# All pieces of w_in loaded before the first recurrence step, and merged transfers for the transposed inverses and the Gram rows, in a fused delta-rule attention and two-MLP kernel

## The chip, the cores and the metric

One core of one Trainium2 chip runs the whole program. The metric is the device time in microseconds of one execution; the kernel before was timed in three runs.

## What is computed

Four batches of eight heads (sequence 768, head width 48) go through a delta rule, and its 3072 rows of 384 features through two MLPs. Cut to what matters:

```python
# attention, per batch and head, t = 0..767
k_n = k / (norm(k) + 1e-6)
y[t]  = q[t] @ state
state = state + beta[t] * outer(k_n[t], v[t] - state.T @ k_n[t])
# first MLP: d_ff = 1024
h = x @ w_in;  solu = h * softmax(h)
x1 = ((solu - mean) / sqrt(var + 1e-6) * g_ln) @ w_out
# second MLP: d_ff = 2048
out = maximum(x1 @ w2_in, 0)**2 @ w2_out
```

The weights arrive as 64-bit floats and everything else as 32-bit floats.

## The kernel before, in words

**Attention.** The 768 tokens of a head are cut into 12 chunks of 64. A *step* t (24 of them, `NT`) holds one chunk of 16 heads-and-batches: 128 partitions by 2 sets by 4 pairs. Steps 0 to 11 and 12 to 23 are two independent recurrences. For every step, **e(t)** multiplies keys with queries and keys (L657); ScalarE puts the negated key-by-key Gram matrix into `g` (L683), which goes to the scratch `gscr` in DRAM, and the masked query part goes to `m`. e runs up to ten steps ahead (`LA`).

A chunk needs the inverse of a 64 by 64 triangular matrix. Its two diagonal 32 by 32 blocks are inverted by forward substitution (`inversion`) for a *group* of four steps at once, all 128 partitions in use, after the blocks have been loaded from `gscr` (into `ia` for group 0, into `it` for the others). The inversion of group 0 runs on VectorE, those of groups 1 to 5 on GpSimd (L886, L868, pairs of L905 and L922, L947 at the end). `it` is stored to `tscr`; ScalarE makes a transposed copy `ia` (L964), which is stored to `uscr`.

`load_tb(t)` brings the pieces of step t back: `g12` (Gram rows), `tbd` (inverses) and `t2` (transposed inverses). The off-diagonal block then takes **prep 1(t)** on TensorE (L1064, g12 by tbd), its copy `ys` by ScalarE (L1070), **prep 2(t)** (L1080, t2 by ys) and four copies into `tbd` (L1093). **z(t)** (L1107) multiplies the finished inverse into m, evacuated to `zs` (L1121). The recurrence itself is **a(t)** (state by keys and queries, L1134 and L1135; none for t = 0 and 12), the residual `r` on VectorE (L1150, or L1152 for t = 0 and 12, from the scaled `vt`), **o(t)** (L1164 and L1165) and the new state `s` (L1180, L1182). The output goes to `xt`.

**First MLP.** **Front(t)** transposes xt (L1206), splits it into a high and a low part `xh`, `xl`, and multiplies with the split w_in: 18 matmuls L1217 into `p_h`, three per 128 by 512 piece of w_in. VectorE takes the row maximum `sc` (L1232), ScalarE the exponential (L1240), VectorE the product with h (L1250); only then is `p_h` free for the next front. **Back** transposes the result (L1319); **out**, for every two fronts, multiplies it with the split w_out (72 matmuls L1339).

**The weights of the first MLP.** `load_w` loads one raw 64-bit piece into one of three `raw` buffers (512 KB for a piece of w_in, 384 KB for one of w_out) and converts it: ScalarE takes the magnitude into one of five `wst` buffers (L453), and four VectorE operations (L461, L472, L487, L497) build the 32-bit float. ScalarE then casts the high part (`w1h`, or `wgh` after a scaling, L534) and GpSimd subtracts for the low part (`w1l`, `wgl`, both L420). VectorE's part may not start before the inversion of group 0 is over (`first_inv`). w_in has six pieces, w_out eight. Two pieces of w_in are loaded before the first `load_tb`, the other four behind it.

**Second MLP.** Its 64-bit weights are converted to DRAM scratch through the same buffers during the attention, and it runs when the attention is over, from about 480 us on.

**What sets the order.** Every operation is added to a `Plan` with a cost, keys that it reads and writes, and a priority from the table `PR`. The plan runs a list scheduler forward and backward over these costs and writes every engine's instructions out in the order found; on the chip each engine then runs its own list strictly in order and waits with semaphores. All transfers go through SyncE (L300), on one hardware queue, in the plan's order.

Of the kernel before, what the change touches and what calls it, by code (L numbers as in the profile page):

```python
# [9 lines left out]
F32 = mybir.dt.float32  # L10
F32R = mybir.dt.float32r
U32 = mybir.dt.uint32
# [6 lines left out]
P = 128  # L19
C = 64  # L20
HB = 32
# [3 lines left out]
NP = 4  # L25
NCH = 12
NST = NB * NCH
GS = 8

G0 = (0, 4, 8, 12, 16, 20, 24)  # L30
NG = len(G0) - 1
# [8 lines left out]
TINY = 1e-36  # L40
RS0 = 2.0**-65.47
LA = 10
NRAW, NWST = 3, 5

F64_LO = 2.0**-15
F64_HI = 2.0**17 * (1 - 2.0**-24)
# [2 lines left out]
def group(t):  # L49
# [5 lines left out]
PR = {  # L55
    "prep": -0.96,
    "z": 0.04,
    "chain": 0.0,
    "e": 0.25,
    "evac": -0.46,  # L60
    "norms": 0.63,
    "inv": -10.66,
    "mf": -1.26,
# [199 lines left out]
def c_dve(n, fast=False):  # L263
    return 0.07 + n / (1920.0 if fast else 960.0)
# [12 lines left out]
def tile_delta_moe_moe(  # L277
# [14 lines left out]
    v, act, pool, pe = nc.vector, nc.scalar, nc.gpsimd, nc.tensor  # L292
# [5 lines left out]
    def dma(dst, src, r=(), w=(), prio=0.0, size=0):  # L298

        return add("sp", 0.06, lambda: nc.sync.dma_start(dst(), src()), r, w, prio, size, gate)  # L300
# [5 lines left out]
    dpool = ctx.enter_context(tc.tile_pool(name="dpool", bufs=1, space=DRAM))  # L306
# [9 lines left out]

    gscr = [dpool.tile([P, GS, NP, C], F32, name=f"gscr{g}") for g in range(NG)]
    tscr = [dpool.tile([4, GS, NP, HB, HB], F32, name=f"tscr{g}") for g in range(NG)]
    uscr = [dpool.tile([4, GS, NP, HB, HB], F32, name=f"uscr{g}") for g in range(NG)]
    x1scr = [dpool.tile([P, 3, 2 * P], F32, name=f"x1scr{i}") for i in range(NT // 2)]  # L320
    w2s = [dpool.tile([P, F2], F32, name=f"w2s{c}") for c in range(3)]
    wos = [dpool.tile([P, DM], F32, name=f"wos{f}") for f in range(16)]
# [40 lines left out]
    ez_ = bufs(m1, [P, F1], "ez", 2)  # L363
# [15 lines left out]
    tbd_ = bufs(ap_, [P, 2 * NP, C], "tbd", 3)  # L379
    t2_ = bufs(ap_, [P, NP, HB], "t2", 2)  # L380
    g12_ = bufs(ap_, [P, 2 * NP, HB], "g12", 2)
    ys = ap_.tile([P, NP, HB], F32, name="ys")
    zs_ = bufs(ap_, [P, NP, 112], "zs", 2)
    R = ap_.tile([P, 2, NP, D], F32, name="r")
    S = ap_.tile([P, 2, NP, D], F32, name="s")
    sqr = [P, HB, HB]
    ia = ap_.tile(sqr, F32, name="ia")
# [6 lines left out]
    raw_ = bufs(ap_, [P, 512, 2], "raw", NRAW, U32)  # L394
# [12 lines left out]
    if 2 * (T2 - T1) < GS:  # L407
        pool.memset(it_[1], 0.0)

    for t in (*tbd_, S, *g12_):  # L410
        pool.memset(t, 0.0)

    def split(hi, lo, src, n, r, w, prio, lo_eng="dve", fast=False):
# [16 lines left out]

    def load_w(src, n, prio):

        i, j = n_w[0] % NWST, n_w[0] % NRAW
        n_w[0] += 1
        w = wst_[i][:, 0:n]
        kw, kr = ("A", "wst", i), ("A", "raw", j)
        if src.dtype == F32:
            dma(lambda: w, lambda: src, (), [kw], prio - 1, P * n * 4)
            return w, kw
        raw, wu = raw_[j][:, 0:n], w.bitcast(U32)  # L440
        up, low = raw[:, :, 1], raw[:, :, 0]
        dma(
            lambda: raw.rearrange("p n t -> p (n t)"),
            lambda: src.bitcast(U32),
            (),
            [kr],
            prio - 1,
            P * n * 8,
        )
        add(  # L450
            "act",
            c_act(n, True),
            lambda: act.activation(out=w, in_=up.bitcast(F32), func=AF.Abs),  # L453
            [kr],
            [kw],
            prio,
        )
        add(
            "dve",
            c_dve(n),  # L460
            lambda: v.scalar_tensor_tensor(  # L461
                out=w, in0=w, scalar=F64_LO, in1=const(3, n), op0=ALU.max, op1=ALU.min
            ),
            [],
            [kw],
            prio,
            after=[*first_inv, *w2_gate],
        )
        add(
            "dve",  # L470
            c_dve(n),
            lambda: v.scalar_tensor_tensor(  # L472
                out=wu,
                in0=wu,
                scalar=3,
                in1=const(5, n, True),
                op0=ALU.logical_shift_left,
                op1=ALU.bitwise_and,
            ),
            [],  # L480
            [kw],
            prio,
        )
# [25 lines left out]
        return w, kw

    def load_w1i(i0, i1, prio):
        for i in range(i0, i1):
            c, n = divmod(i, 2)
            s = slice(n * 512, n * 512 + 512)
            w, kw = load_w(w1i[c, :, s], 512, prio)
            split(
                lambda c=c, s=s: w1h[:, c, s],
                lambda c=c, s=s: w1l[:, c, s],
                lambda w=w: w,
                512,  # L520
                [kw],
                [("W", "w1h", c, n), ("W", "w1l", c, n)],
                prio,
                "pool",
            )
# [303 lines left out]

    def inversion(g, en, prio):  # L830

        eng, cost = (v, lambda n, full=True: c_dve(n)) if en == "dve" else (pool, c_pool)
        gm = gm_[g % 2]
        it, itmp = it_[g % 2], junk[:, 512:] if g == 1 else itmp_
        kgm, kic, kia = ("A", "gm", g % 2), ("A", "itc", g % 2), ("A", "ia")
# [60 lines left out]
        for j in range(1, HB - 1):  # L896
# [69 lines left out]
            [kia, *(kraws if g == 0 else ())],  # L966
            prio,
        )
        dma(
            lambda: uscr[g].rearrange("h g p r s -> (h g p) r s"),  # L970
            lambda: ia,
            [kia],
            [("A", "uscr", g)],
            prio,
            P * 4096,
        )

    def load_tb(t, prio):

        g, tg = group(t)  # L980
        s0 = 2 * tg
        tb, t2, g12 = tbd_[t % 3], t2_[t % 2], g12_[t % 2]
        ktb, kt2, kg12 = ("A", "tbd", t % 3), ("A", "t2", t % 2), ("A", "g12", t % 2)
        for h in range(2):
            o = h * C
            dma(
                lambda o=o: g12[o : o + HB],
                lambda o=o: gscr[g][o : o + HB, s0 : s0 + 2].rearrange("r s p c -> r (s p) c")[
                    :, :, HB:
                ],  # L990
                [("A", "gscr", g, s) for s in (s0, s0 + 1)],
                [kg12 + (h,)],
                prio - 1,
                2 * HB * 1024,
            )

        def blk(scr, hb):
            return scr[g][hb, s0 : s0 + 2].rearrange("s p r c -> r (s p) c")

        for hb in (0, 2, 1, 3):  # L1000
            o, c = hb * HB, hb % 2 * HB
            last = dma(
                lambda o=o, c=c: tb[o : o + HB, :, c : c + HB],
                lambda hb=hb: blk(tscr, hb),
                [("A", "tscr", g)],
                [ktb + (hb,)],
                prio - 1,
                2 * 32 * 1024,
            )
        for h in range(2):  # L1010
            for e in range(2):
                o = (2 * h + e) * HB
                dma(
                    lambda o=o: t2[o : o + HB],
                    lambda h=h, e=e: uscr[g][2 * h + 1, s0 : s0 + 2].rearrange(
                        "s (k e) r c -> e r (s k) c", e=2
                    )[e],
                    [("A", "uscr", g)],
                    [kt2 + (h, e)],
                    prio - 1,  # L1020
                    2 * 32 * 512,
                )
        return last

    def load_kv(t, prio):
# [31 lines left out]
    def prep1_mm(t):  # L1057
        tb, g12 = tbd_[t % 3], g12_[t % 2]

        def mm():  # L1060
            for u in range(2 * NP):
                for h in range(2):
                    o, q = h * C, (2 * h + u % 2) * HB
                    pe.matmul(yp[q : q + HB, u // 2], g12[o : o + HB, u], tb[o : o + HB, u, 0:HB], start=True, stop=True)  # L1064

        r = [*(("A", "g12", t % 2, h) for h in range(2)), *(("A", "tbd", t % 3, 2 * h) for h in range(2))]
        return mm, r, [("A", "a")]

    def prep1_out(t, prio):
# [2 lines left out]
    def prep2_mm(t):  # L1072
        t2 = t2_[t % 2]

        def mm():
            for u in range(2 * NP):
                for h in range(2):
                    q = (2 * h + u % 2) * HB
                    s = slice(q, q + HB)
                    pe.matmul(yp[s, u // 2], t2[s, u // 2], ys[s, u // 2], start=True, stop=True)  # L1080

        return mm, [("A", "ys"), *(("A", "t2", t % 2, h, e) for h in range(2) for e in range(2))], [("A", "a")]

    def prep2_out(t, prio):
        tb = tbd_[t % 3]
# [493 lines left out]

    gate.append(wr)  # L1580
    inversion(1, "pool", PR["inv1"])
    load_w1i(0, 2, PR["w1i"])
    for t in range(T2, LA):
        e_tile(t, PR["e1"] + t * PR["e1s"])
        norms(t, PR["n2"])
# [10 lines left out]
    load_tb(1, PR["prep0"] + 2)  # L1596
    load_kv(1, PR["prep0"] + 2)
    prep_z(1, PR["prep0"] + 2, (1,))
    load_w1i(2, 6, PR["w1i"])
    load_w1o(PR["w1o"])  # L1600
    for t in range(NT + 3):
        if t < NT:
# [149 lines left out]
```

## Time and profile before

| | |
|---|---|
| Three runs | 905.94, 906.82, 912.15 us; median 906.82 |
| The profiled execution | 916.59 us, of which the span is 914.9 us |
| TensorE busy | 817.2 us (89% of the span) |
| VectorE, ScalarE, GpSimd busy | 499.5, 449.9, 311.2 us |
| Mean granted TensorE clock | 0.946 |
| DMA | 99.72 MB in 126576 packets, 84225 of them under 512 bytes |

A line of the page names an engine, a line of the kernel and the tiles. "Idle before" is the time the engine stood still before an instruction, with what released it. TensorE's clock (PEclk) is a share of 2.4 GHz; at 0.5 it runs at 1.2 GHz.

### The profile page before, as it was taken

How to read it: one execution, taken by the hardware profiler on the slowest of the kernel's cores; microseconds unless marked ns; L12 is line 12 of the kernel's file. 1: busy time of each engine (PE TensorE's matmuls, PEld its weight loads, DVE VectorE, ACT ScalarE, POOL GpSimd, SP SyncE). 2: the span in 40 equal slices, each digit the busy share in tenths (PEclk: the TensorE clock that was granted, in tenths of full speed). 3: DMA queues.
4: the chain of work that ended last, by engine and by line, in shares of the span. 5: the costliest groups of instructions: out<-in, count | busy, mean ns of one | idle time of the engine just before them, and what ended most of it. 6: DMA issues, size and time to landing. Idle time of an engine off the chain costs nothing.

```text
span 914.9 us, 24277 instructions
## 1 busy us (share of the span) xinstructions
PE 817.2 (89%) x9904; PEld 757.4 (83%) x9904; DVE 499.5 (55%) x984; ACT 449.9 (49%) x996; POOL 311.2 (34%) x759
## 2 busy tenths in 40 slices
PE   5425858999979889988999999999999999999997
PEld 4324647888868677787888999999999999999997
DVE  4994898543875875665657454343433333343332
ACT  2313587685766656475667444343333334343333
POOL 4389978757988957930000000000000000000000
PEclk9975877999999998998999999999999999999999
DMA  9826887456786775556434421010100101010101
GB/s 229 216 73 173 220 232 196 133 156 149 196 266 168 206 205 148 158 155 160 145 93 142 113 79 52 1 53 1 39 14 1 52 1 52 1 27 1 27 1 26
DMA packets 126576, 99.72 MB, mean 109 GB/s; under 512 B 84225, under 2 KB 106753, under 8 KB 126465
## 3 DMA queue, kind: packets, MB, share of 16 engines
q1 hardware_dynamic: 126464, 98.18, 39.2%
q8 instruction: 77, 1.26, 0.6%
q14 instruction: 35, 0.28, 0.1%
HBM read 69.83 MB, written 28.31 MB: 107 GB/s over the span
## 4 chain that ended last, share of the span: by engine, by line
PE 66%; DVE 12%; DMA 7%; POOL 4%; ACT 4%; issue 3%; SPq 3%; ACTq 0%; DVEq 0%; POOLq 0%
PE acc L1526 21%; PE h L1482 21%; PE p_x L1339 7%; PE p_h L1217 7%; SPq L300 3%; PE p_tr L1319 2%; PE p_a L1134 2%; DVE wst L461 2%; DVE itmp L905 2%; POOL it L922 1%; POOL itmp L905 1%; DVE it L922 1%; DVE wst L487 1%; DMA raw<-in_w1i_dram 1%; PE p_u L1107 1%
## 5 line engine op out<-in xcount | busy, mean ns | idle before, releaser
L1503 DVE TENSOR_TENSOR xt<-xt 128x384 f32<-128x384 f32 x128 | 71.5, 559 | 166.4 <-ACT xt L1495 166.3
L1495 ACT ACTIVATE xt<-h 128x384 f32<-128x384 f32 x128 | 62.8, 491 | 166.3 <-PE h L1482 165.9
L1482 PE MATMUL h<-x1l,w2h 128*128 128x384 f32 x384 | 128.7, 335 | 0.0
L1482 PE MATMUL h<-x1h,w2h 128*128 128x384 f32 x384 | 128.6, 335 | 0.0
L1482 PE MATMUL h<-x1h,w2l 128*128 128x384 f32 x384 | 128.5, 335 | 0.0
L1339 PE MATMUL p_x<-zh,wgh 128*128 128x256 f32 x288 | 87.3, 303 | 5.8 <-ACT xo L1353 5.4
L922 POOL TENSOR_TENSOR it<-it,itmp 128x72 f32<-128x72 f32 (+37 forms) x204 | 88.2, 448 | 4.5
L1526 PE MATMUL acc<-woh,xh 128*128 128x384 f32 x258 | 87.7, 340 | 0.9 <-ACT ot L1548 0.9
L905 POOL TENSOR_TENSOR itmp<-it 128x72 f32<-128x72 f32 (+37 forms) x204 | 86.9, 441 | 2.0
L1526 PE MATMUL acc<-wol,xh 128*128 128x384 f32 x258 | 87.4, 339 | 0.0
L1526 PE MATMUL acc<-woh,xl 128*128 128x384 f32 x258 | 87.1, 338 | 0.0
L1339 PE MATMUL p_x<-zh,wgl 128*128 128x256 f32 x288 | 83.2, 289 | 2.2 <-issue 2.2
L1339 PE MATMUL p_x<-zl,wgh 128*128 128x256 f32 x288 | 83.4, 290 | 0.3 <-DVE zl L420 0.3
L420 DVE TENSOR_TENSOR xl<-xt,xh 128x384 fp32r<-128x384 f32 x86 | 48.0, 558 | 44.8 <-ACT xh L415 44.4
L1482 PEld LDWEIGHTS h<-x1h,w2h 128*128 128x128 f32 x384 | 72.1, 188 | 0.0
L1482 PEld LDWEIGHTS h<-x1h,w2l 128*128 128x128 f32 x384 | 72.1, 188 | 0.0
L1482 PEld LDWEIGHTS h<-x1l,w2h 128*128 128x128 f32 x384 | 72.1, 188 | 0.0
L415 ACT CAST xh<-xt 128x384 fp32r<-128x384 f32 x86 | 44.1, 513 | 48.2 <-DVE xt L1503 47.2
L1217 PE MATMUL p_h<-w1h,xh 128*128 128x512 f32 x144 | 64.5, 448 | 2.6 <-DVE xl L420 2.6
L1339 PEld LDWEIGHTS p_x<-zh,wgh 128*128 128x128 f32 x288 | 56.4, 196 | 9.2 <-ACT xo L1353 6.2
L1217 PE MATMUL p_h<-w1l,xh 128*128 128x512 f32 x144 | 59.6, 414 | 0.0
L1217 PE MATMUL p_h<-w1h,xl 128*128 128x512 f32 x144 | 59.4, 413 | 0.0
(179 smaller groups left out, 1985.4 us busy)
## 6 DMA issues: line engine op xcount, KB each, us to landing
kql<-in_kin_dram SPq DMA_DIRECT2D x22, 512.0 KB, 5.1
kqe<-in_kin_dram SPq DMA_DIRECT2D x38, 192.0 KB, 3.0
raw<-in_w2i_dram SPq DMA_DIRECT2D x12, 512.0 KB, 5.3
raw<-in_w2o_dram SPq DMA_DIRECT2D x16, 384.0 KB
gscr<-g SPq DMA_DIRECT2D x21, 256.0 KB, 5.8
m<-in_ktok_dram SPq DMA_DIRECT2D x24, 192.0 KB, 6.8
vt<-in_vtok_dram SPq DMA_DIRECT2D x24, 192.0 KB, 3.9
x1scr<-xo SPq DMA_DIRECT2D x12, 384.0 KB, 3.7
```

The lines of the kernel that those rows point to most:

```text
L300: return add("sp", 0.06, lambda: nc.sync.dma_start(dst(), src()), r, w, prio, size, gate)
L415: add("act", c_act(n), lambda: act.copy(hi(), src()), r, [w[0]], prio)
L420: lambda: le.tensor_tensor(out=lo(), in0=src(), in1=hi().bitcast(F32), op=ALU.subtract),
L461: lambda: v.scalar_tensor_tensor(out=w, in0=w, scalar=F64_LO, in1=const(3, n), op0=ALU.max, op1=ALU.min),
L905: lambda tm=tm, j=j, nr=nr, w_=w_, c0=c0, c1=c1: eng.tensor_tensor(out=tm, in0=it[:, j + 1 :, j : j + 1].to_broadcast([P, nr, w_]), in1=it ...
L922: lambda tm=tm, j=j, c0=c0, c1=c1: eng.tensor_tensor(out=it[:, j + 1 :, c0:c1], in0=it[:, j + 1 :, c0:c1], in1=tm, op=ALU.add,),
L1217: pe.matmul(p_h[:, sl], xx[:, c], ww[:, c, sl], start=(c == 0 and k == 0), stop=(c == 2 and k == 2),)
L1339: pe.matmul(p_x1[:, 0 : 2 * P], ww[:, f, c * P : c * P + P], zz[:, f], start=(f == 0 and k == 0), stop=(f == 7 and k == 2),)
L1482: pe.matmul(late["h2", ih], late[ww][:, c, s], xx[:, c], start=(c == 0 and k == 0), stop=(c == 2 and k == 2),)
L1495: lambda: act.activation(out=rt, in_=late["h2", ih], func=AF.Relu),
L1503: lambda: v.tensor_tensor(out=gg, in0=rt, in1=rt, op=ALU.mult),
L1526: pe.matmul(late["acc", a], gg[:, a * P : a * P + P], late[ww][:, f], start=(f == 0 and k == 0), stop=(f == 15 and k == 2),)
```

## The change

- **w_in:** all six raw pieces are loaded ahead of the first `load_tb`. Pieces 0 to 3 go to four `raw` buffers (`NRAW` 3 to 4), pieces 4 and 5 to `ez_0` and `ez_1`, which hold inputs of e(4) and e(5) before and the first MLP's exponentials later. There are four `wst` buffers instead of five.
- **Transposed inverses:** `uscr` is laid out as t2 needs it. The store is two transfers of 128 KB (only the two blocks that are used) in pieces of 128 bytes, where it was one of 512 KB in pieces of 4 KB. t2 of a step is one transfer of 128 rows of 512 bytes, where it was four with pieces of 128 bytes.
- **Gram rows:** g12 of a step is one transfer over all 128 partitions (128 KB, half of it unused rows), where it was two of 32 KB. g12 is no longer set to zero at the start.
- **Plan:** the cost that the plan reckons for a VectorE operation of an inversion is 0.09 higher. `PR` is unchanged.

```diff
-NRAW, NWST = 3, 5
+NRAW, NWST = 4, 4
...
-    uscr = [dpool.tile([4, GS, NP, HB, HB], F32, name=f"uscr{g}") for g in range(NG)]
+    uscr = [dpool.tile([P, GS * NP // 2, HB], F32, name=f"uscr{g}") for g in range(NG)]
...
-    for t in (*tbd_, S, *g12_):
+    for t in (*tbd_, S):
...
-        i, j = n_w[0] % NWST, n_w[0] % NRAW
+        i, j = n_w[0] % NWST, n_w[0] - NRAW
         n_w[0] += 1
         w = wst_[i][:, 0:n]
-        kw, kr = ("A", "wst", i), ("A", "raw", j)
+        if 0 <= j < 2:
+            raw, kr = ez_[j].bitcast(U32).rearrange("p (n t) -> p n t", t=2)[:, 0:n], ("ez", j)
+        else:
+            j = (j - 2) % NRAW if j > 0 else j + NRAW
+            raw, kr = raw_[j][:, 0:n], ("A", "raw", j)
+        kw = ("A", "wst", i)
...
-        eng, cost = (v, lambda n, full=True: c_dve(n)) if en == "dve" else (pool, c_pool)
+        eng, cost = (v, lambda n, full=True: c_dve(n) + 0.09) if en == "dve" else (pool, c_pool)
...
-        dma(
-            lambda: uscr[g].rearrange("h g p r s -> (h g p) r s"),
-            lambda: ia,
...
+        for h in range(2):
+            o = (2 * h + 1) * HB
+            dma(
+                lambda h=h: uscr[g][rows[h]].rearrange("(e r) k c -> k e r c", e=2),
+                lambda o=o: ia[o : o + HB],
...
-        for h in range(2):
-            o = h * C
-            dma(
-                lambda o=o: g12[o : o + HB],
...
+        dma(
+            lambda: g12,
+            lambda: gscr[g][:, s0 : s0 + 2, :, HB:].rearrange("r s p c -> r (s p) c"),
...
-        for h in range(2):
-            for e in range(2):
-                o = (2 * h + e) * HB
-                dma(
-                    lambda o=o: t2[o : o + HB],
...
+        dma(
+            lambda: t2,
+            lambda: uscr[g][:, s0 * NP // 2 : s0 * NP // 2 + NP],
...
     inversion(1, "pool", PR["inv1"])
-    load_w1i(0, 2, PR["w1i"])
+    load_w1i(0, 6, PR["w1i"])
...
-    load_w1i(2, 6, PR["w1i"])
     load_w1o(PR["w1o"])
```

The plan writes a new order for every engine. Line numbers of the changed kernel are up to five off those of the kernel before (L457 to L953 are five higher there, L1044 and later two or three lower).

**SyncE's queue, the stretch ahead of the load of group 1's Gram blocks** (`it_1<-gscr1`), first as it stands before:

```order
L300 DMA raw_0_213<-in_w1i_dram 128x1024
L300 DMA gscr1_76<-g_1_178 128x512
L300 DMA kqe_0_175<-in_kin_dram 48x1024 x2
L300 DMA gscr1_76<-g_0_177 128x512
L300 DMA kqe_1_176<-in_kin_dram 48x1024
L300 DMA raw_1_214<-in_w1i_dram 128x1024
L300 DMA kqe_1_176<-in_kin_dram 48x1024
L300 DMA m_8_173<-in_ktok_dram 128x2x192
L300 DMA m_9_174<-in_ktok_dram 128x2x192
L300 DMA it_1_205<-gscr1_76 32x32x32 x4
```

In the changed kernel, from the third piece of w_in on (the two rows ahead of these are `raw_0` and `raw_2` from w_in):

```order
L300 DMA raw_3_216<-in_w1i_dram 128x1024
L300 DMA kqe_0_175<-in_kin_dram 48x1024 x2
L300 DMA gscr1_76<-g_0_177 128x512
L300 DMA kqe_1_176<-in_kin_dram 48x1024
L300 DMA gscr1_76<-g_1_178 128x512
L300 DMA raw_1_214<-in_w1i_dram 128x1024
L300 DMA kqe_1_176<-in_kin_dram 48x1024
L300 DMA m_8_173<-in_ktok_dram 128x2x192
L300 DMA m_9_174<-in_ktok_dram 128x2x192
L300 DMA ez_0_157<-in_w1i_dram 128x1024
L300 DMA ez_1_158<-in_w1i_dram 128x1024
L300 DMA it_1_205<-gscr1_76 32x32x32 x4
```

Six pieces of w_in now stand ahead of the four block loads, where two stood.

**ScalarE, after the transposed copy of group 0's inverse** (`ys` is the copy between prep 1 and prep 2 of step 0, then of step 1). Before:

```order
L964 COPY ia_203<-it_0_204 128x32x32
L415 CAST w1h_163<-wst_1_217 128x512
L415 CAST w1h_163<-wst_0_216 128x512
L1070 COPY ys_198<-p_a_223 128x128
L1093 COPY tbd_0_191<-p_a_223 32x4x32 x4
L1121 COPY zs_0_199<-p_u0_221 128x448
L1121 COPY zs_1_200<-p_u1_222 128x448
```

In the changed kernel:

```order
L969 COPY ia_203<-it_0_204 128x32x32
L415 CAST w1h_163<-wst_0_217 128x512
L415 CAST w1h_163<-wst_1_218 128x512
L458 ACTIVATE wst_0_217<-ez_0_157 128x512
L1068 COPY ys_198<-p_a_223 128x128
L415 CAST w1h_163<-wst_2_219 128x512
L1091 COPY tbd_0_191<-p_a_223 32x4x32 x4
L458 ACTIVATE wst_1_218<-ez_1_158 128x512
L415 CAST w1h_163<-wst_3_220 128x512
L1068 COPY ys_198<-p_a_223 128x128
L415 CAST w1h_163<-wst_0_217 128x512
L1119 COPY zs_0_199<-p_u0_221 128x448
```

The magnitude of piece 4, which overwrites `wst_0`, now stands ahead of step 0's `ys`, and so it can go only when GpSimd's subtraction for piece 0 has read `wst_0`.

**GpSimd, the end of group 1's inversion** (`it_1`, products in `junk`), in the changed kernel; before, none of the rows on `it_0` (group 2's inversion) stands ahead of the end of group 1's:

```order
L420 TENSOR_TENSOR wgl_145<-wst_2_219,wgh_144 128x384
L910 TENSOR_TENSOR junk_159<-it_1_205 128x18
L910 TENSOR_TENSOR junk_159<-it_1_205 128x40
L891 TENSOR_TENSOR it_0_204<-it_0_204,gm_0_209 128x1024
L927 TENSOR_TENSOR it_1_205<-it_1_205,junk_159 128x2x9
L873 AFFINE_SELECT it_0_204<-it_0_204 128x1024
L927 TENSOR_TENSOR it_1_205<-it_1_205,junk_159 128x2x20
L910 TENSOR_TENSOR itmp_206<-it_0_204 128x30
```

Ahead of the last operation of group 1's inversion there now stand five of the `wgl` subtractions, L891 and L873 and seven operations of group 2's inversion, which stood behind it. The first `w1l` subtraction stands behind two more pairs of rounds of the inversion than before.

**Other places.** On VectorE the 24 conversions of w_in follow the end of group 0's inversion in nearly one run; before, eight did. On TensorE the two orders have the same matmuls ahead of o(4) (72 of L1217, 48 of L1339); ahead of o(3) the changed one has 42 of L1339, the one before 6. From step 4 on, the matmuls ahead of each step's o differ by no more than 24 of L1339.

## Rows read from the trace of the kernel before

**Rows 1.** Windows: us; busy PE, PEld, DVE, ACT, POOL; PEclk; DMA share; GB/s.

```profile
480.00:915.00 435.00, 427.17 (x2489) 425.20 (x2489) 176.25 (x308) 172.10 (x337) 0.00 (x0) 1.00 0.13 36
```

**Rows 2.** VectorE's waits from 60 to 160 us: total us, times, longest.

```profile
DVE wst L461 <- ACT wst L453: 11.6, 4, 7.0
```

**Rows 3.** Windows of 5 us while group 1's Gram blocks are loaded.

```profile
30.00:35.00 5.00, 0.33 (x8) 0.22 (x8) 4.45 (x14) 0.79 (x4) 1.18 (x2) 1.00 0.68 144
35.00:40.00 5.00, 2.13 (x29) 1.74 (x32) 4.49 (x18) 0.66 (x1) 0.00 (x0) 1.00 1.00 299
40.00:45.00 5.00, 2.92 (x42) 1.99 (x35) 4.97 (x25) 2.40 (x7) 0.00 (x0) 1.00 1.05 212
```

**Rows 4.** GpSimd in time: start, us, what, last [idle before <- releaser].

```profile
47.98 3.69 POOL L886 TENSOR_TENSOR it<-it,gm 128x1024 f32<-128x1024 f32 x1 [16.80 <-DMA it<-gscr]
70.36 1.27 POOL L420 TENSOR_TENSOR w1l<-wst,w1h 128x512 fp32r<-128x512 f32 x1 [2.44 <-ACT w1h L415]
120.37 2.33 POOL L947 TENSOR_TENSOR it<-it,gm 128x1024 f32<-128x1024 f32 x1
123.09 1.00 POOL L420 TENSOR_TENSOR wgl<-wst,wgh 128x384 fp32r<-128x384 f32 x1 [0.39 <-ACT wgh L415]
124.07 2.68 POOL L886 TENSOR_TENSOR it<-it,gm 128x1024 f32<-128x1024 f32 x1
129.40 1.26 POOL L868 TENSOR_SCALAR_AFFINE_SELECT it<-it 128x1024 f32<-128x1024 f32 x1
202.99 2.38 POOL L886 TENSOR_TENSOR it<-it,gm 128x1024 f32<-128x1024 f32 x1 [6.38 <-ACT gm L814]
```

**Rows 5.** The page's costliest groups: one operation of GpSimd's inversions.

```profile
L922 POOL TENSOR_TENSOR it<-it,itmp 128x72 f32<-128x72 f32 (+37 forms) x204 | 88.2, 448 | 4.5
```

**Rows 6.** VectorE in time: the maximum of front 0, the last conversion of w_out.

```profile
113.94 1.21 DVE L1232 TENSOR_REDUCE sc<-p_h 128x1 f32<-128x1024 f32 x1
153.61 0.79 DVE L497 SCALAR_TENSOR_TENSOR wst<-raw,wst 128x384 uint32<-128x384 uint32 x1
```

**Rows 7.** TensorE in time: o(0), and the first matmul of front 2.

```profile
82.82 0.31 PE L1164 MATMUL p_a<-r,zs 64*48 64x48 f32 x1 [1.16 <-ACT tbd L1093]
137.22 0.80 PE L1217 MATMUL p_h<-w1h,xh 128*128 128x512 f32 x1 [0.62 <-DVE xl L420]
```

**Rows 8.** The chain of waits: start, us, what; the last row shown is o(4).

```profile
127.67 5.31 DMA uscr<-ia
165.26 2.87 PE p_x L1339 x24
168.13 0.17 PE p_a L1164
```

**Rows 9.** Windows of 10 us up to o(4).

```profile
130.00:140.00 10.00, 5.05 (x16) 3.05 (x14) 10.00 (x15) 8.77 (x21) 7.73 (x16) 0.70 0.63 182
140.00:150.00 10.00, 9.40 (x280) 7.61 (x280) 9.37 (x16) 6.91 (x17) 8.89 (x15) 0.96 0.60 149
150.00:160.00 10.00, 7.90 (x149) 6.86 (x149) 6.18 (x11) 7.96 (x21) 8.91 (x24) 0.73 0.83 246
160.00:170.00 10.00, 10.00 (x151) 8.86 (x154) 3.07 (x5) 5.44 (x11) 9.69 (x33) 0.93 0.37 100
```

**Rows 10.** The line of the transposed copy: duration ns min/median/max.

```profile
L964 ACT COPY ia<-it x6: 1920/2054/2122, 64.3 to 403.3; 128x1024 f32<-128x1024 f32 x6
```

**Rows 11.** DMA issues: count, KB each, median us to landing; last a window from 324 us.

```profile
it<-gscr SPq DMA_DIRECT2D x20, 128.0 KB, 3.1
t<-uscr SPq DMA_DIRECT2D x96, 16.0 KB, 1.8
uscr<-ia SPq DMA_DIRECT2D x1, 512.0 KB, 7.4
```

**Rows 12.** SyncE's issues in time: the t2 transfers of two steps.

```profile
278.65 3.77 SPq L300 DMA_DIRECT2D t<-uscr  x8
```

**Rows 13.** TensorE in time: a wait at the end of group 3's inversion.

```profile
267.44 0.58 PE L1339 MATMUL p_x<-zh,wgh 128*128 128x256 f32 x1 [4.18 <-ACT xo L1353]
```

More of the change, by code (lines that the diff above doesn't have):

```diff
@@ L439, in load_w @@
             return w, kw
-        raw, wu = raw_[j][:, 0:n], w.bitcast(U32)
+        wu = w.bitcast(U32)
         up, low = raw[:, :, 1], raw[:, :, 0]
@@ L968, in inversion @@
         )
-        dma(
-            lambda: uscr[g].rearrange("h g p r s -> (h g p) r s"),
-            lambda: ia,
[L972 to L976, printed above, removed]
+        for h in range(2):
[3 more added lines that the diff above has]
+                lambda o=o: ia[o : o + HB],
+                [kia],
+                [("A", "uscr", g, h)],
+                prio,
+                P * 1024,
+            )
     def load_tb(t, prio):
@@ L983, in load_tb @@
         ktb, kt2, kg12 = ("A", "tbd", t % 3), ("A", "t2", t % 2), ("A", "g12", t % 2)
-        for h in range(2):
-            o = h * C
-            dma(
-                lambda o=o: g12[o : o + HB],
[L988 to L995, printed above, removed]
+        dma(
+            lambda: g12,
+            lambda: gscr[g][:, s0 : s0 + 2, :, HB:].rearrange("r s p c -> r (s p) c"),
+            [("A", "gscr", g, s) for s in (s0, s0 + 1)],
+            [kg12],
+            prio - 1,
+            P * 1024,
+        )
         def blk(scr, hb):
@@ L1009, in load_tb @@
             )
-        for h in range(2):
-            for e in range(2):
-                o = (2 * h + e) * HB
-                dma(
-                    lambda o=o: t2[o : o + HB],
[L1015 to L1022, printed above, removed]
+        dma(
+            lambda: t2,
+            lambda: uscr[g][:, s0 * NP // 2 : s0 * NP // 2 + NP],
+            [("A", "uscr", g, h) for h in range(2)],
+            [kt2],
+            prio - 1,
+            P * 512,
+        )
         return last
@@ L1064, in mm @@
                     pe.matmul(yp[q : q + HB, u // 2], g12[o : o + HB, u], tb[o : o + HB, u, 0:HB], start=True, stop=True)
-        r = [*(("A", "g12", t % 2, h) for h in range(2)), *(("A", "tbd", t % 3, 2 * h) for h in range(2))]
+        r = [("A", "g12", t % 2), *(("A", "tbd", t % 3, 2 * h) for h in range(2))]
         return mm, r, [("A", "a")]
@@ L1080, in mm @@
                     pe.matmul(yp[s, u // 2], t2[s, u // 2], ys[s, u // 2], start=True, stop=True)
-        return mm, [("A", "ys"), *(("A", "t2", t % 2, h, e) for h in range(2) for e in range(2))], [("A", "a")]
+        return mm, [("A", "ys"), ("A", "t2", t % 2)], [("A", "a")]
     def prep2_out(t, prio):
```

## The prediction

> **What bounds the kernel now.** I read the page first: TensorE is busy 89% of the span, but unevenly. The windows show the second MLP full, 427 of 435 us [rows 1], and nothing in the change reaches it. So I looked for stretches in which TensorE starves. The largest lies between 64 and 160 us, after the inversion of group 0 and before the first MLP has its weights. There the chain of waits runs through VectorE and the raw pieces, and VectorE's waits name the cause: 11.6 us for the magnitude of a piece whose raw data had just landed [rows 2]. What this delays can be read off TensorE: front 2 starts at 137.22 us, the last conversion of w_out starts at 153.61, o(4) starts at 168.13 [rows 6 to 8]. The windows between 137.2 and 168.1 give TensorE's work there: busy time by granted clock, 2.8 x 0.5 + 9.4 x 0.96 + 7.9 x 0.73 + 8.1 x 0.93 = 23.7 us at full clock in 30.9 us (0.5 because front 2 begins at 1.2 GHz) [rows 7 to 9]. So 7.2 us are lost there. Both orders have the same matmuls ahead of o(4), and nearly the same ahead of every later o; the time of o(4) therefore measures the change.
>
> **1. Early pieces: the gain.** With all six raw pieces in SBUF, VectorE converts w_in without the waits of rows 2, up to 11.6 us. It then reaches w_out earlier, and the plan puts 36 more matmuls of the first out (L1339) ahead of o(3). The last conversion of w_out moves from 153.6 to about 138: minus 11.6, minus some 5 us of recurrence and front-2 work now queued behind it, plus the wait under 3 of about 1.
>
> **2. Early pieces: the cost in the queue.** Four more pieces, 2.1 MB, now go ahead of group 1's Gram blocks. That stretch is DMA-bound: a share of 1.0 at 212 to 299 GB/s, with only 0.32 of 5 us unused ahead of it [rows 3]. 2.1 MB take 7.0 to 9.9 us, less at most 1.6: 5.4 to 9.9. I take 7, by the higher rate, since these are large contiguous rows. GpSimd, which had waited 16.8 us for those blocks and started group 1's inversion at 47.98 [rows 4], starts it at 55. GpSimd has little other idle time from there to 120 us, so everything on its queue moves by 7.
>
> **3. GpSimd's queue makes the start later.** The first w1l subtraction began at 70.36 after 2.44 us of waiting [rows 4]. Now it follows the inversion's rounds, two pairs more, eight operations at 0.45 [rows 5]: 67.9 + 7 + 3.6 = 78.5, end 79.8. The magnitude of piece 4 needs its buffer, and on ScalarE step 0's ys stands behind that magnitude. So ys goes at about 80.5, VectorE waits some us for piece 4, and prep 2, z, zs and o(0) follow. I let o(0) start at 88 to 89 instead of 82.82 [rows 7], also because e(10) now stands ahead of it. But e(10) is done by then, and no wait for weights is left inside front 0. Its maximum, at 113.94 [rows 6], therefore comes 0 to 6 us later. I take 1.1, near the low end, because o(0)'s delay and the waits removed nearly cancel. Fronts 1 and 2 follow one after the other through p_h, so front 2 starts at 138.3.
>
> **4. From front 2 to o(4).** The weights of w_out are ready (138, plus scale, cast and subtraction about 2.5). Without gaps the 23.7 us of work, plus 1.4 because front 2's first 2.8 us are again at half clock, end at 163.4. That is 4.7 earlier than 168.1.
>
> **5. Is group 1's inverse there in time?** It ended at 122.7. Plus 7 for the start; plus what the plan puts ahead of the end: five wgl at 1.0, L886 2.68, L868 1.26, seven operations at 0.45 [rows 4, 5], 12.1; minus the idle 2.44 that a later GpSimd no longer meets: 139.4. The transposed copy takes 2.05 [rows 10], the store 5.3 [rows 8], a t2 transfer 1.8 to land and 0.5 to issue [rows 11, 12]: prep 2 of step 4 can go at 149.0. TensorE reaches it at 138.3 + 4.3 (18 matmuls of 512 columns at the rate of 24 of 256 in 2.87, rows 8) + 1.4 + 2.9 + about 1.5 for a prep 1 and a(3) = 148.4. It waits 0.6, and o(4) comes at 164.0.
>
> **6. The uscr store in 128-byte pieces.** No row shows such a store to DRAM. From below: a transfer of 1024 pieces of 128 bytes, read from DRAM, lands in 3.1, and the store is two of 1024; so it can also land 2.2 earlier than the old one. From above: twice the longest landing of the old store, 14.8 [rows 11]. I take 5.3, the old store's time on the chain [rows 8], as the row with pieces of the same size lies much nearer to it than to 14.8; both ends go into the range. The Trainium skill, DMA: Bandwidth & Descriptors, Specifications, states that transfers under 512 bytes are read, modified and written back instead of running at line rate. By it the store would lie toward the upper end and rival D would get its case; this trace has only reads of such pieces, at 3.1 us, which don't settle it.
>
> **7. Fewer transfers.** 72 t2 and 24 g12 transfers go, 6 stores come; a t2 issue takes 3.77 / 8 = 0.47 us [rows 12]. That frees some 42 us of SyncE's queue, spread over 24 steps, where TensorE is hardly waiting for these tiles. At the four later group boundaries a burst of eight becomes two, 2.8 us. Between 0 and 3 us in all reach TensorE; I take 0, since its other work covers them. The extra bytes of g12 (64 KB a step) and two memsets are hidden under e's early lead. The 0.09 in the plan costs nothing by itself: its effect is the order, counted above.
>
> **Sum.** 168.1 - 164.0 = 4.1 us off the profiled execution: 916.6 to 912.5. That execution lies 1.1% over the median of the runs, and the change is a difference; so the forecast is 906.8 - 4.1 = **902.7**.
>
> **The rivals.**
> *B, the full gain, 896.* The Gram blocks don't come later, because the queue absorbs the pieces. Then the 5.8 us of step 3 fall away too, and o(4) moves by about 10.5 (4.7 + 5.8; the inverse is ready at 142). For it: ahead of the blocks the queue was idle for part of the time, and what I call 7 may be 5.4. Against: the pieces stand ahead of the blocks in the queue's order, at full share [rows 3].
> *C, no change, 907.* The gain is given back later: ScalarE waits for group 3's inversion and TensorE stood 4.18 us behind it [rows 13]; if that inversion ends no earlier, the 4.1 us are lost there. Against: it starts on a product that follows TensorE's own progress (GpSimd waited 6.38 for it, rows 4).
> *D, slower, 915.* Group 1's inverse becomes the bound at prep 2 of step 4. It decides once that can go only after 148.4 + 4.7 = 153.1. With the late start at 9.9 (2.9 more) and the store at 14.8 (9.5 more) it goes at 161.4, o(4) 15 us behind it (163.4 - 148.4) at 176.4: 8.3 slower, 915; five wgl waits on GpSimd's queue (0.39 each, rows 4) add 2. For it: GpSimd's queue is full, and the plan puts group 2's work ahead of group 1's end. Against: the two unknowns must both be near their upper ends. The page named under 6 speaks for it.
>
> **Chances.** Forecast 0.43 (897 to 906, by the 5.4 to 9.9 of step 2 and the 0 to 6 of step 3), B 0.28, C 0.15, D 0.14. The range 891 to 914 takes in B with up to 3 us from step 7 and a good part of D. A measurement of this kernel can tell about 1% from no change, 9 us: faster than 897.8 is most of B and an edge of the forecast, 0.31; slower than 915.9 is half of D and what I overlook, 0.11; within, 0.58.
>
> **What would show it.** VectorE's waits for raw pieces should be gone, with a wait of a few us at piece 4 in their place. Group 1's first GpSimd operation should start near 55 us (48: B). Step 0's ys should come near 80, front 0's maximum near 115, the last conversion of w_out near 138, the end of group 1's inversion near 139, o(4) near 164. A TensorE wait ahead of prep 2 of step 4 of over 5 us is D; o(4) earlier and the end not is C. The forecast is wrong if the load of the blocks is not bandwidth-bound, or if the fronts don't set the pace between 114 and 137.

## The result, and the profile after

The changed kernel takes 896.31 us (median of four runs, 895.35 to 900.25), against 907.72 for the kernel before in the same comparison: a ratio of 0.9873 (95% interval 0.9829 to 0.9918), 11.4 us less. A second comparison, in more rounds, gave 0.9878 (0.9827 to 0.9929). The forecast was 902.7, a gain of 4.1: right in direction and inside the range, but too small by 7 us.

One caution for all that follows. Single executions of the kernel before lay between 902.75 and 918.99 us, and its profiled one (916.59) near the upper end. So verdicts below are ratios with their intervals, and traces are compared in pairs or over several executions.

Windows of the changed kernel: us; busy PE, PEld, DVE, ACT, POOL; PEclk; DMA share; GB/s. They answer to [rows 1], [rows 3] and [rows 9].

```profile
30.00:35.00 5.00, 0.33 (x8) 0.19 (x8) 4.69 (x12) 2.20 (x8) 3.05 (x3) 1.00 0.91 296
35.00:40.00 5.00, 2.09 (x30) 1.81 (x34) 4.73 (x19) 1.32 (x2) 0.00 (x0) 1.00 1.04 330
40.00:45.00 5.00, 1.94 (x39) 1.54 (x34) 5.00 (x27) 2.49 (x7) 0.00 (x0) 1.00 1.04 310
...
130.00:140.00 10.00, 4.47 (x29) 3.17 (x19) 8.13 (x14) 7.82 (x15) 9.97 (x22) 0.66 0.57 202
140.00:150.00 10.00, 10.00 (x182) 8.84 (x180) 3.60 (x5) 8.75 (x16) 8.61 (x22) 1.00 0.46 91
150.00:160.00 10.00, 9.35 (x295) 8.13 (x283) 2.29 (x5) 5.41 (x18) 8.03 (x26) 1.00 0.81 197
160.00:170.00 10.00, 10.00 (x259) 8.86 (x260) 4.62 (x9) 6.96 (x18) 9.55 (x33) 1.00 0.49 132
...
480.00:890.00 410.00, 408.12 (x2362) 407.42 (x2360) 161.37 (x284) 157.23 (x310) 0.00 (x0) 1.00 0.11 31
```

The second MLP is full as before. The load queue now runs at a share of 1.04 up to 45 us. TensorE starves until 140 and then holds the full clock, where before it sank to 0.73 between 150 and 160.

The milestones that the prediction named, from the changed kernel's engines in time (start, us, what, last [idle before <- releaser]); they answer to [rows 4], [rows 6] and [rows 7].

```profile
50.89 2.41 POOL L891 TENSOR_TENSOR it<-it,gm 128x1024 f32<-128x1024 f32 x1 [17.84 <-DMA it<-gscr]
...
75.60 1.26 POOL L420 TENSOR_TENSOR w1l<-wst,w1h 128x512 fp32r<-128x512 f32 x1
...
77.47 0.25 ACT L1068 COPY ys<-p_a 128x128 f32<-128x128 f32 x1
...
77.59 1.32 DVE L466 SCALAR_TENSOR_TENSOR wst<-wst,cst 128x512 f32<-128x512 f32 x1 [6.78 <-ACT wst L458]
...
114.92 1.21 DVE L1230 TENSOR_REDUCE sc<-p_h 128x1 f32<-128x1024 f32 x1
...
135.47 0.62 DVE L502 SCALAR_TENSOR_TENSOR wst<-raw,wst 128x384 uint32<-128x384 uint32 x1
...
136.27 1.91 POOL L952 TENSOR_TENSOR it<-it,gm 128x1024 f32<-128x1024 f32 x1
...
149.64 0.45 PE L1078 MATMUL p_a<-ys,t 32*32 32x32 f32 x32
...
162.66 0.24 PE L1162 MATMUL p_a<-r,zs 64*48 64x48 f32 x1
```

Forecast and found: GpSimd's start on group 1 55 and 50.9; first w1l 78.5 and 75.6; ys 80.5 and 77.5; front 0's maximum 115 and 114.9; last conversion 138 and 135.5; inverse of group 1 done 139.4 and 138.2; prep 2(4) 149.0 and 149.6; o(4) 164.0 and 162.7. Two more executions in the change's order have o(4) at 165.4 and 161.7; a second one of the kernel before has it at 168.7, by [rows 8] it was at 168.1. So o(4) came about 5 us earlier, for a forecast of 4.1. Whether this lead is part of the 11.4 us is taken up behind the experiments.

The changed kernel's stores of transposed inverses (count, KB each, median us to landing), answering to [rows 11]:

```profile
uscr<-ia SPq DMA_DIRECT2D x12, 128.0 KB, 2.6
```

### The profile page after: what moved, and what is told of

Same layout as the page of the kernel before. It is cut to its first block, busy times and chain, and to the rows that moved or that the text cites. A ratio compares the mean times of both kernels' runs of the same rounds, so it can differ in the third digit from the quotient of the medians.

```text
span 893.7 us, 24147 instructions
## 1 busy us (share of the span) xinstructions
PE 800.9 (90%) x9904; PEld 746.3 (84%) x9904; DVE 490.3 (55%) x984; ACT 449.3 (50%) x996; POOL 317.0 (35%) x757
## 4 chain that ended last, share of the span: by engine, by line
PE 64%; DVE 11%; POOL 8%; DMA 7%; ACT 5%; issue 3%; SPq 2%; ACTq 0%; POOLq 0%; DVEq 0%
PE acc L1524 22%; PE h L1480 22%; PE p_x L1337 7%; PE p_h L1215 6%; POOL it L927 3%; DMA raw<-in_w2i_dram 2%; POOL itmp L910 2%; SPq L300 2%; PE p_tr L1317 1%; POOL junk L910 1%; DVE wst L492 1%; PE p_a L1132 1%; DVE wst L502 1%; DVE zl L420 1%; DVE wst L466 1%
## 5 line engine op out<-in xcount | busy, mean ns | idle before, releaser
L910 POOL TENSOR_TENSOR itmp<-it 128x72 f32<-128x72 f32 (+37 forms) x204 | 89.3, 453 | 2.0
L420 DVE TENSOR_TENSOR xl<-xt,xh 128x384 fp32r<-128x384 f32 x86 | 47.9, 558 | 46.3 <-ACT xh L415 46.1
L1215 PE MATMUL p_h<-w1h,xh 128*128 128x512 f32 x144 | 62.2, 432 | 1.4 <-DVE xl L420 1.4
```

What stands on the lines that cost most here:

```text
L420: lambda: le.tensor_tensor(out=lo(), in0=src(), in1=hi().bitcast(F32), op=ALU.subtract),
L910: lambda tm=tm, j=j, nr=nr, w_=w_, c0=c0, c1=c1: eng.tensor_tensor(out=tm, in0=it[:, j + 1 :, j : j + 1].to_broadcast([P, nr, w_]), in1=it ...
L1215: pe.matmul(p_h[:, sl], xx[:, c], ww[:, c, sl], start=(c == 0 and k == 0), stop=(c == 2 and k == 2),)
```

## The experiments

All ratios are to the kernel before on the same chip, five rounds each, with 95% intervals. "Old order" means that every engine's list is that of the kernel before, and only the transfers differ: the plan is run as before, and an operation then issues other transfers.

**1. The kernel before once more.** No edit.

> The kernel before, unchanged, for a second profile: its first profiled execution took 916.6 us, 9 us over the median of its other runs, so a comparison of milestones with it may show 9 us too much. If that execution was late by chance, this one takes 905 to 910 us and the last front of the first MLP ends near 483 us instead of 491.9. If the profiler itself costs 9 us on this kernel, it takes 914 to 918 again with the same milestones.

Measured: 1.0015 (0.9983 to 1.0047); the profiled execution took 914.09 us, front 23's maximum at 489.2. The second expectation fits the time better, but the profiler is not the cause: executions without it reached 918.99, and the changed kernel's profiled one (896.41) lies on its median. A difference of under some 10 us between the totals of two single executions says little here.

**2. Order and transfers crossed.** New order with old transfers, and old order with new ones:

```diff
 # new order, old transfers: one operation issues what four issued
-            lambda: t2,
-            lambda: uscr[g][:, s0 * NP // 2 : s0 * NP // 2 + NP],
+        def four():
+            for h in range(2):
+                for e in range(2):
+                    nc.sync.dma_start(t2[o : o + HB], uscr[g][2 * h + 1, ...
 # old order, new transfers: the first of four operations issues all
+                def one_(h=h, e=e):
+                    if h == e == 0:
+                        nc.sync.dma_start(t2, uscr[g][:, s0 * NP // 2 : s0 * NP // 2 + NP])
```

> The changed kernel with its own order of instructions on every engine, but each merged transfer put back in its place: one contiguous uscr store, four t2 and two g12 transfers a step. Theory 1 (the gain is made by the early pieces and the new order, the transfers cost nothing): 895 to 898 us, ratio 0.985 to 0.990. Theory 2 (the 7 us beyond the forecast come from the shorter bursts of transfers at the later group boundaries): 901 to 905 us, ratio 0.993 to 0.998, with TensorE waits on tbd, g12 or t2 near 240 to 270, 310 to 350 and 385 to 430 us.

> The kernel before with its own order on every engine, and only the transfers of the change: uscr stored in 128-byte pieces, one t2 and one g12 transfer a step. Theory 1: 905 to 909 us, ratio 0.998 to 1.002. Theory 2: 900 to 903 us, ratio 0.991 to 0.995. If the store in 128-byte pieces were slow (14.8 us, rival D's upper bound), group boundaries would come some 10 us later and the kernel would be slower than 910.

Measured: new order with old transfers 1.0106 (1.0062 to 1.0149), slower than before; old order with new transfers 0.9899 (0.9861 to 0.9937). Theory 1 falls. Theory 2 had 0.993 to 0.998 for the first kernel and missed it too; its 0.991 to 0.995 for the second overlaps with the interval. The TensorE waits that it named are not there: in those stretches the first kernel waits 1.0 us for tbd, and not for g12 or t2. The transfers are worth 9.2 us in the old order and some 21 us in the new one (0.988 against 1.011 of 910), which the plan had made for the new transfers.

Where they act shows in the new order with either kind of transfer: the two kernels have the same lists on TensorE, VectorE and ScalarE. SyncE in time at the boundary to group 1 (start, us, transfers); the changed kernel:

```profile
142.01 2.30 SPq L300 DMA_DIRECT2D tbd<-tscr  x4
144.43 0.38 SPq L300 DMA_DIRECT2D t<-uscr  x1
144.85 0.92 SPq L300 DMA_DIRECT2D tbd<-tscr  x2
145.81 0.45 SPq L300 DMA_DIRECT2D t<-uscr  x1
...
151.21 0.38 SPq L300 DMA_DIRECT2D vt<-in_vtok_dram  x1
...
160.08 0.42 SPq L300 DMA_DIRECT2D vt<-in_vtok_dram  x1
```

With the old transfers in the same order:

```profile
142.58 1.85 SPq L300 DMA_DIRECT2D tbd<-tscr  x4
144.53 1.83 SPq L1013 DMA_DIRECT2D t<-uscr  x4
146.40 0.93 SPq L300 DMA_DIRECT2D tbd<-tscr  x2
147.38 2.68 SPq L1013 DMA_DIRECT2D t<-uscr  x4
...
155.32 0.38 SPq L300 DMA_DIRECT2D vt<-in_vtok_dram  x1
...
166.90 1.55 SPq L300 DMA_DIRECT2D vt<-in_vtok_dram  x1
```

SyncE issues one transfer after another, so whatever stands behind the burst comes later: the first vt by 4.1 us (0.6 of it because the burst itself began later), the next by 6.8. From 155 to 300 us, waits of GpSimd and ScalarE for such loads (total us, times, longest) are twice as long. The changed kernel:

```profile
POOL vt L1042 <- DMA vt<-in_vtok_dram: 16.3, 6, 6.3
...
ACT sq L750 <- DMA m<-in_ktok_dram: 6.3, 5, 2.6
```

With the old transfers:

```profile
POOL vt L1042 <- DMA vt<-in_vtok_dram: 31.9, 7, 8.2
...
ACT sq L750 <- DMA m<-in_ktok_dram: 12.5, 5, 6.9
```

From 155 to 300 us no wait of TensorE is put down to a transfer in either kernel. Its waits for ScalarE come to 13.2 us with the old transfers and to 5.4 in the changed kernel; that these go back to the late loads is read from the waits, not tested by itself. TensorE's windows, the changed kernel first:

```profile
160.00:200.00 40.00, 39.40 (x849) 34.20 (x849) 21.49 (x49) 28.81 (x71) 26.18 (x87) 1.00 0.63 164
200.00:240.00 40.00, 40.00 (x916) 34.65 (x909) 24.65 (x46) 26.48 (x67) 34.85 (x96) 1.00 0.67 181
```

```profile
160.00:200.00 40.00, 37.34 (x692) 32.65 (x693) 20.08 (x45) 23.77 (x59) 27.70 (x95) 0.91 0.66 178
200.00:240.00 40.00, 36.21 (x780) 31.81 (x772) 15.59 (x28) 24.82 (x62) 26.23 (x72) 0.91 0.50 121
```

Busy time times granted clock is 79.4 us in the one and 66.9 in the other: with the old transfers TensorE is busy for 5.9 us less, and the granted clock of the stretch is 0.91 instead of 1.00.

**3. Which transfers, and is it their number or their pieces?** Old order; t2 in one transfer, t2 in four of the new layout (512 bytes a row), g12 in one.

```diff
 # t2 in four, new layout
-                    if h == e == 0:
-                        nc.sync.dma_start(t2, uscr[g][:, s0 * NP // 2 : s0 * NP // 2 + NP])
+                    nc.sync.dma_start(t2[o : o + HB], uscr[g][o : o + HB, c0 : c0 + NP])
```

> The kernel before in its own order, with the new uscr layout (stored in 128-byte pieces) and one t2 transfer a step; g12 stays at two. The whole set of new transfers in this order took 9.2 us off (ratio 0.9899, 0.9861 to 0.9937). Theory 1 (the number of transfers in SyncE's queue counts): t2 takes away 72 of the 96 issues, so 6 to 8 us, ratio 0.991 to 0.994. Theory 2 (the two g12 transfers matter as much, each standing at the head of a step's loads): 3 to 5 us, ratio 0.995 to 0.997.

> As the run with one t2 transfer, new uscr layout too, but t2 is loaded by four transfers of 32 partitions each, one run of 512 bytes a partition; the number of issues on SyncE is that of before (two more for the stores). Theory 1 (number of issues): no gain, ratio 0.998 to 1.002. Theory 3 (size of the pieces: the old t2 transfers read 128-byte pieces): most of the gain of the one transfer stays, ratio 0.991 to 0.995.

> The kernel before in its own order, with g12 in one transfer of all 128 partitions in place of two of 32; uscr and t2 as before. Theory 1: 24 of the 96 issues, 1 to 3 us, ratio 0.997 to 0.999, less what 64 KB more a step cost (24 steps). Theory 2: 4 to 6 us, ratio 0.993 to 0.996.

Measured: t2 in one 0.9915 (0.9885 to 0.9945), in four 1.0017 (0.9984 to 1.0049), g12 in one 0.9957 (0.9928 to 0.9985). With four transfers of the new layout the gain is gone: the size of the pieces and the store's layout together are worth nothing measurable, and the gain goes with the number of issues. 72 fewer for t2 (with six more for the stores) gave 7.7 us, as theory 1 had it; 24 fewer for g12 gave 3.9, between theory 1 (1 to 3) and theory 2 (4 to 6), with an interval that covers both, so where an issue stands may count too. The two together make 11.6, and both at once gave 9.2; the intervals allow that. SyncE at the boundary to group 2, t2 in one:

```profile
192.68 3.96 SPq L300 DMA_DIRECT2D tbd<-tscr  x6
196.74 0.87 SPq L1013 DMA_DIRECT2D t<-uscr  x2
...
205.57 0.36 SPq L300 DMA_DIRECT2D vt<-in_vtok_dram  x1
```

and in four:

```profile
196.81 3.75 SPq L300 DMA_DIRECT2D tbd<-tscr  x6
200.61 3.70 SPq L1013 DMA_DIRECT2D t<-uscr  x8
...
212.40 0.37 SPq L300 DMA_DIRECT2D vt<-in_vtok_dram  x1
```

From the first tbd to vt: 12.9 and 15.6 us. The six issues less are 2.7 us at one boundary. There are five, 13.5 us of queue if they are alike, and 9.3 us lie between the two kernels (0.0102 of 911).

**4. The early pieces.** In the old order, without and with the new transfers, and the change's own plan without them:

```diff
 # old order: the four loads are moved in the finished order
+        want = [i for i in plan.order() if i not in early[2:6]]
+        for a, b in ((early[2], early[0]), (early[3], early[2])):
+            want.insert(want.index(b) + 1, a)
+        first = min(want.index(i) for i in it1)
+        want[first:first] = early[4:6]
 # merged transfers only, without the 0.09, ordered anew by the plan
-NRAW, NWST = 4, 4
+NRAW, NWST = 3, 5
...
-        eng, cost = (v, lambda n, full=True: c_dve(n) + 0.09) if en == "dve" else (pool, c_pool)
+        eng, cost = (v, lambda n, full=True: c_dve(n)) if en == "dve" else (pool, c_pool)
...
-    load_w1i(0, 6, PR["w1i"])
+    load_w1i(0, 2, PR["w1i"])
...
+    load_w1i(2, 6, PR["w1i"])
```

> The kernel before with its own order on every engine, and only the loads of pieces 2 to 5 moved ahead of group 1's Gram blocks, into the buffers that the change gives them. If the waits for raw data are what cost the time (step 1 of the prediction), VectorE's four waits fall to one at piece 4, and the time is 898 to 904 us, ratio 0.989 to 0.996. If the gain comes from the order that the plan finds once the pieces are early (normalisation of group 0 first, group 1's inversion later beside group 0's), it is 905 to 911 us, ratio 0.998 to 1.004, group 0's inversion ending near 64 us as before.

> The kernel before in its own order with both parts of the change: all new transfers, and pieces 2 to 5 loaded ahead of group 1's Gram blocks. In the same order the transfers alone gave 0.9899 (0.9861 to 0.9937) and the early pieces alone 1.0021. Theory 1: 0.988 to 0.992, no better than the transfers alone. Theory 4: 0.983 to 0.987, some 4 us better.

> The changed kernel without its early pieces and without the 0.09 in the plan's cost: only the merged transfers, and the plan knows of them and orders everything anew. The changed kernel has 0.9873 (0.9829 to 0.9918). Theory 1 (the transfers are the whole gain, the early pieces are worth nothing measurable): 0.985 to 0.991. Theory 4 (the early pieces need the shorter queue to pay; they bring the 3 to 4 us of the prediction's start-up steps): 0.990 to 0.994, at or above the old order with new transfers (0.9899).

> The changed kernel once more, beside the next three and in more rounds: its first comparison (0.9873, 0.9829 to 0.9918) overlaps with the merged transfers alone (0.9922, 0.9893 to 0.9951). Theory 1 (the early pieces add nothing): 0.989 to 0.993. Theory 4 (they add the 3 to 5 us of the start-up once the queue is shorter): 0.984 to 0.989.

Measured: early pieces alone 1.0021 (0.9989 to 1.0054); both parts 0.9917 (0.9889 to 0.9944), against 0.9899 for the transfers alone; the plan with merged transfers only 0.9922 (0.9893 to 0.9951); the change again 0.9878. In a fixed order the early pieces are worth nothing measurable. In the plan's order the kernel with merged transfers only lies some 4 us behind the change (0.9922 against 0.9876, the mean of the change's two comparisons), with intervals that overlap; but it lacks the 0.09 as well as the pieces. Only the pieces separate it from the kernel of experiment 5, which has them and no 0.09: 0.9982 (0.9956 to 1.0008). There the pieces come with a loss of 5.5 us, and the two intervals just fail to meet. What the pieces are worth beside the 0.09, no run shows.

VectorE's waits from 60 to 160 us, beside [rows 2], show what stands in the way of a gain. The kernel with early pieces alone:

```profile
DVE r L1167 <- POOL vt L1059: 7.0, 1, 7.0
DVE r L1165 <- POOL idle L950: 4.8, 2, 3.8
...
DVE wst L474 <- ACT wst L466: 2.2, 2, 1.6
```

The kernel before, whose only wait for GpSimd in this view is

```profile
DVE r L1152 <- POOL vt L1044: 4.1, 1, 4.1
```

The 11.6 us for raw pieces are down to 2.2, as expected, and the waits for GpSimd have gone from 4.1 to 11.8 us. GpSimd's start had moved, since the pieces go ahead of its Gram blocks.

**5. The 0.09.** The change without it.

```diff
-        eng, cost = (v, lambda n, full=True: c_dve(n) + 0.09) if en == "dve" else (pool, c_pool)
+        eng, cost = (v, lambda n, full=True: c_dve(n)) if en == "dve" else (pool, c_pool)
```

> The changed kernel without the 0.09 that the change adds to the plan's cost of VectorE's inversion steps; everything else as in the change, ordered anew by the plan. The prediction gave the 0.09 no cost of its own. If that holds: within 0.003 of the changed kernel. If the 0.09 is what puts group 0's inversion first (it ended some 6 us earlier than in the kernel before): 0.005 or more slower than the changed kernel.

Measured: 0.9982 (0.9956 to 1.0008), 9.6 us slower than the change. But group 0's inversion is as early without the 0.09 (its last product at 57.15 us; 56.26 with it), so the reason that I expected is wrong. The difference shows at group 1: GpSimd's list has all eight `wgl` subtractions of w_out ahead of the end of the inversion instead of five, and ScalarE's transposed copy comes late. GpSimd, ScalarE and a window of the kernel without the 0.09:

```profile
142.57 1.92 POOL L952 TENSOR_TENSOR it<-it,gm 128x1024 f32<-128x1024 f32 x1
...
145.37 1.94 ACT L969 COPY ia<-it 128x1024 f32<-128x1024 f32 x1
```

```profile
138.00:172.00 34.00, 26.25 (x579) 23.31 (x579) 8.49 (x14) 17.25 (x39) 28.24 (x85) 0.90 0.54 134
```

The same of the changed kernel:

```profile
138.51 2.08 ACT L969 COPY ia<-it 128x1024 f32<-128x1024 f32 x1
```

```profile
138.00:172.00 34.00, 33.35 (x770) 29.07 (x771) 13.14 (x25) 25.12 (x59) 30.19 (x89) 0.98 0.61 156
```

Busy time times clock: 23.6 against 32.7 us, so 9.1 us lie between the two in this stretch, close to the 9.6 of the ratios; it is one pair of traces. The inverse is 6.3 us late, as rival D feared, in a kernel that differs by one number in the plan's cost. But D's wait is not the one that it causes: ahead of prep 2 of step 4 TensorE waits under 2 us, and its longest wait, 3.80 us at 148.30, is for an operation on the exponentials (L1258) that stands right behind the late copy on ScalarE.

**6. One step further: kqe in one transfer.**

```diff
+                if t < LA:
+                    nc.sync.dma_start(kq[f], kin[f, 2 * t : 2 * t + 2])
+                elif h == 0:
+                    nc.sync.dma_start(kq, kin[:, 2 * t : 2 * t + 2])
```

> The changed kernel in its own order, and from step 10 on kqe is loaded by one transfer of 128 partitions in place of two of 48: 14 fewer issues on SyncE, 128 KB more a step (1.8 MB in all, partitions that nothing reads). Theory 1 (each issue taken from SyncE's queue is worth some 0.1 to 0.16 us: 9.2 us for 90 issues net, 3.9 us for 24 of g12): 1.4 to 2.3 us faster than the changed kernel, about 0.002 lower in ratio. Rival (only the issues in the bursts at the group boundaries count, and kqe stands outside them; the extra bytes cost): no change or up to 2 us slower.

Measured: 0.9884 (0.9844 to 0.9923), against 0.9878 for the change beside it. No gain shows; 0.002 would not have been told from none. No version beat the change.

## Why the prediction was right in direction and too small

**Step 7 failed, in its size.** It priced the transfers taken away right (0.47 us an issue, 2.8 a burst), and then took 0, with at most 3 in all, "since its other work covers them". The runs show 9.2 us (5.7 to 12.7) for just this part in the old order. Two errors are in the step. The 2.8 of one burst was made the bound of all of them, though the step itself counted four boundaries: 4 x 2.8 is 11. And I looked for the cover on TensorE, whose waits for t2 came to 0.6 us, instead of at what is queued behind the burst on SyncE: tbd of the following steps, vt, m. Experiments 2 and 3 show vt and m late.

**The measure failed too.** The prediction let the time of o(4) stand for the whole change. The first o(4) of two other kernels, the new order with old transfers and the plan with merged transfers only:

```profile
162.71 0.24 PE L1162 MATMUL p_a<-r,zs 64*48 64x48 f32 x1
```

```profile
171.21 0.24 PE L1157 MATMUL p_a<-r,zs 64*48 64x48 f32 x1
```

The one is as early as in the change, and its kernel is 1.1% slower than the kernel before; the other is later than in the kernel before, and its kernel is 0.8% faster. In the old order without early pieces o(4) lies anywhere from 160.9 to 168.7 in six traces, with old transfers, new ones or some of each. From o(4) to the end of the span it takes 747 and 744 us in the two traces of the kernel before and 760 in the new order with old transfers; 732 in the old order with new transfers, 733 with both parts, and 731 to 735 in three traces in the change's order. So the merged transfers act mainly behind o(4), where the sum had nothing. Whether any of the lead at o(4) reaches the end, no run separates. The forecast of 4.1 was made of that lead alone, so that it had the right direction is in part luck.

**Step 1 came out at its place, but by other terms.** The last conversion came at 135.5 for a forecast of 138, yet the 11.6 us of VectorE's waits that were to go are still 10.6. VectorE's waits from 60 to 160 us and ScalarE's magnitude of piece 4, in the changed kernel:

```profile
DVE wst L466 <- ACT wst L458: 10.6, 4, 6.8
```

```profile
76.90 0.66 ACT L458 ACTIVATE wst<-ez 128x512 f32<-128x512 f32 x1 [12.06 <-POOL w1l L420]
```

The raw data is there in time, but ScalarE stands 12.06 us for the buffer that GpSimd's first subtraction has to read, and 6.78 of them become VectorE's wait at piece 4, where the step took about 1. VectorE went from its first conversion to its last in 64.5 to 154.4 us before and in 57.7 to 136.1 now. The 18.3 us are a start 6.8 earlier (the end of group 0's inversion, for which the sum had no term; see the last section), 6.3 less work in between, and 5.1 less idle time, only 1.0 of it at the magnitudes.

**Steps 3 to 5 held as places and times,** to within about 3 us each (milestones above): front 2 started at 137.74 for a forecast of 138.3, and o(4) came out at 161.7 to 165.4 for 164.0. But a gain of the early pieces is shown by no run. Alone, in the old order, they trade VectorE's waits for GpSimd's, and with the plan's order but without the 0.09 they come with a loss. The prediction read the actual order and so had the 0.09 in its times, while its words gave the gain to the pieces and nothing to the 0.09, without which the change loses 9.6 us.

**Step 2** took 7 us for the later Gram blocks. GpSimd's first product of group 1 started at 44.8 to 48.0 us (mean 46.3) in seven executions with late pieces, at 50.8 to 53.4 (mean 51.8) in seven with early ones: 5.5, the lower end of the step's 5.4 to 9.9. The step missed what it gives back on VectorE (below). **Step 6** took 5.3 us for the store in 128-byte pieces; from 110 to 480 us it landed in 2.6 (median; 3.9 to 5.9 in three kernels of the old order), the old store in 7.4. The Trainium skill, DMA: Bandwidth & Descriptors, Specifications, states that transfers under 512 bytes are read, modified and written back; here such a store of 128 KB landed no later than one of 512 KB in long rows, and by t2 in four the layout as a whole cost nothing measurable. Whether they are slower byte for byte, no run here separates.

**The rivals.** The time is B's (896), but not by B: the blocks did come later. C's giving back did not happen to the change, whose lead grew behind o(4). It may be what happened to the early pieces alone (o(4) at 163.2, total unchanged), but that rests on one trace, within the 160.9 to 168.7 above. D did not happen in the changed kernel (TensorE reached prep 2(4) when it was ready, 149.6). Experiment 5 shows a lateness of the inverse like D's one constant of the plan away; it takes back what the change gains (0.9982) and does not reach D's 915.

## What to carry to other kernels

A single in-order queue that issues transfers is an engine like the others: price the burst at every place where it recurs, and look for the loss at what is queued behind it, not at the consumer of the transfers merged. When a scheduler reorders everything, cross the two parts (new order with old operations, old order with new ones) before crediting either. A milestone early in the span measures a change only if its lead is shown to last to the end. A wait taken away on one engine is a gain only if the engine behind it was not waiting too.

## What was not expected of the hardware

VectorE and GpSimd slow each other when both invert. The same VectorE pair beside GpSimd's inversion (kernel before) and while GpSimd still waits for its blocks (changed kernel):

```profile
57.67 0.63 DVE L905 TENSOR_TENSOR itmp<-it 128x36 f32<-128x36 f32 x2
```

```profile
50.52 0.33 DVE L910 TENSOR_TENSOR itmp<-it 128x36 f32<-128x36 f32 x2
```

The sharpest case is the next such pair in the changed kernel. It is smaller, but it starts while GpSimd's first product runs (from 50.89 for 2.41 us, above):

```profile
51.02 2.43 DVE L910 TENSOR_TENSOR itmp<-it 128x27 f32<-128x27 f32 x2
```

GpSimd's first product took 3.7 to 6.0 us in seven executions with late pieces, and 2.3 to 2.4 in seven with early ones, where it falls beside VectorE's last, small steps. Group 0's inversion on VectorE, from its first product to the end of its last, took 30.7 to 32.2 us (mean 30.9) in the former and 26.4 to 28.1 (mean 27.5) in the latter. So the later Gram blocks cost GpSimd 5.5 us at its start, and VectorE's inversion was 3.4 shorter. The Trainium skill, SBUF — State Buffer, Who interferes with whom, states that a VectorE instruction with two SBUF inputs contends with a GpSimd instruction that reads SBUF; these rows agree.
